# Gate and value products of layer 1 as a 2x2 block product with seven products, in the list scheduler's order

## The chip, the cores and the metric

One core of one Trainium2 chip runs the whole program. The metric is the time of one execution in device microseconds; three runs of a kernel give its median. Engine names: PE (TensorE, matrix products), DVE (VectorE), ACT (ScalarE), POOL (GpSimd), SP (SyncE, which here only issues DMAs). SBUF is the on-chip memory, PSUM the eight banks into which PE writes.

## What is computed

Attention with a threshold, then two layers in sequence. Cut to what matters here:

```
x = attention(q, k, v, tau)                  # 2304 tokens x 512
rms = sqrt(mean(x * x, axis=-1) + 1e-6)
xn = x / rms * rms_g
g = xn @ w_gate                              # 512 -> 1536
val = xn @ w_val                             # 512 -> 1536
x = (silu(g) * val) @ w_out                  # layer 1: 1536 -> 512
h = x @ w_in                                 # layer 2: 512 -> 2048
out = (h * cos(h)) @ w_out2                  # 2048 -> 512
```

Every factor is held as a high part (fp32r) and a low part (what is left), and a product is three matmuls: high by high, high by low, low by high.

## The kernel before

Tokens stand in six chunks of 384 (`TC`, `NCH`), with the model dimension on the partitions in four k-tiles of 128 (`KD`). Layer 1 has twelve column tiles of 128 for gate and value (`F1`), in six groups of two (`G1`). The loop goes over groups, in a group over chunks, in a chunk over the two tiles; one such step is a *unit* (72 in all, `seq`). A unit runs `gv_mm` twice, once for gate and once for value: four k-tiles by three matmuls each, 24 matmuls of 128x128 by 128x384 into tile `pgv` (two banks). Then ACT takes the silu (`h_silu`), DVE multiplies by value (`h_mul`), ACT makes the high part of h (`h_hi`) and DVE the low part (`h_lo`). `px_mm` multiplies h by the output weights: 12 matmuls into four banks `px`; after the second tile of a group `px_out` adds them to `acc`, in SBUF (four DVE adds of 128x384; in the first group four ACT copies).

Weights come as 64-bit floats. `weight_job` loads 512 KB (`raw`), turns it into 32 bit (two DVE steps, one ACT step and one POOL step on `wtmp`) and splits it (`whi` by ACT, `wlo` by DVE). Each weight tile is loaded and split once.

Two things set the order of the instructions. The attention, the first four units' gate and value products, the first two units' output products and the x of chunks 0 to 3 are steps of a `Plan`: a list scheduler with a cost in ns for each kind of step (`STEPS`), counted buffers (`take`, `free`), and a third number per kind that says which of the steps that could start goes first. It also keeps the steps in `LOCK` (DVE and POOL steps that use a common path to SBUF) from overlapping, by its own costs, and makes the POOL steps in `BEHIND` wait for the DVE step ahead. The rest of layer 1 and all of layer 2 are written out by hand: `pump` advances up to three weight jobs between units, and layer 1 sends unit n's output products behind unit n+1's gate and value products. Each engine works its own list in order; SP's DMAs are one queue.

Of the kernel before, what the change touches and what calls it, by code (L numbers as in the profile page):

```python
# [9 lines left out]
F32 = mybir.dt.float32  # L10
# [8 lines left out]
P = 128  # L19
# [57 lines left out]
    "j_a": ("ACT", 540, -8083508),
    "gv": ("PE", 2090, -3245104),
    "silu": ("ACT", 420, -5068320),
    "px": ("PE", 2090, 3553935),  # L80
    "pxc": ("ACT", 400, 54632),
    "hmul": ("DVE", 480, -8051011),
    "hhi": ("ACT", 420, -838003),
    "hlo": ("DVE", 480, 3843445),
# [5 lines left out]
    "mask", "j1", "j2", "x_d", "hlo", "th", "div", "sq", "x_add", "rms", "radd", "x_p", "j_p",  # L90
}
BEHIND = {"div", "sq", "x_add", "x_p", "j_p"}
# [9 lines left out]
N_EARLY = 4  # L102
N_PX = 2
# [111 lines left out]
def attention_moe_cos_kernel(  # L215
# [36 lines left out]
    w_a = ctx.enter_context(tc.tile_pool(name="w_a", bufs=6))  # L252
    x0_p = ctx.enter_context(tc.tile_pool(name="x0", bufs=1))
    xs = {}
# [41 lines left out]

    def weight_job(n, key, pool, stage, src, idle):
# [29 lines left out]
        hi = pool.tile([P, 4, P], F32R, tag="whi", name="whi")  # L327
        lo = pool.tile([P, 4, P], F32R, tag="wlo", name="wlo")
# [396 lines left out]
    def x_halves(c):  # L725
        if c not in xs:
            hi, lo = (late[c].tile([P, KD, TC], F32R, tag=t, name=t) for t in ("xh", "xl"))
            xs[c] = [(hi[:, kk], lo[:, kk]) for kk in range(KD)]
        return xs[c]
# [9 lines left out]
    def x_scale(c, kk):  # L739
        nc.gpsimd.tensor_tensor(acc[c, kk], acc[c, kk], xrs[c], op=ALU.mult)  # L740
# [87 lines left out]

    def px_out(g, c, d):
        dst = acc[c][:, d]  # L830
        if g == 0:
# [13 lines left out]

    def attention():
# [4 lines left out]
            "x0": 2, "jraw": 1, "jtmp": 1, "hh": 2, "one": 1,  # L851
        })
# [136 lines left out]
        def chunk(c, at, tiles, rs_tile, after, free):  # L989
# [6 lines left out]
            for kk in range(KD):  # L996
# [3 lines left out]
                x = add("x_p", at, x_scale, c, kk, after=[x, r])  # L1000
# [37 lines left out]
        def grow_2():  # L1038
            att_s.close()
            late[2] = ctx.enter_context(tc.tile_pool(name="xhl2", bufs=1, side="right"))  # L1040
            late["acc", 3] = late["acc", 0] = ctx.enter_context(
                tc.tile_pool(name="acc3", bufs=2, side="right")
            )
            late["rs", 3] = ss_p
# [10 lines left out]
        e2 = {}  # L1055

        def e_tile(i):
            if i not in e2:
                e2[i] = e_p.tile([P, 2, S], F32, tag="e", name="xe")
            return e2[i]  # L1060

        x2 = chunk(
            2, NU + 5, lambda kk: e_tile(kk // 2)[:, kk % 2, 0:TC], lambda: e_tile(2)[:, 0, 0:TC],
            [g2], [[("e", ("e2", 2))], [("e", ("e2", 0))], [], [("e", ("e2", 1))], [], [[]] * KD],
        )
        x = add("x_load", NU + 6, load_x, 3, after=[g2, done["rs", 2]] + x0 + [done[x] for x in range(8, 12)])
        add("x_p", NU + 6, scale_x, 3, after=[x])
        hs = []
        for n in range(N_EARLY):
            c = seq[n][1]  # L1070
            x = add("gv", NU + n, gv_mm, n, 0, after=(x0, x1)[c] + jops + [smm[NU - 1], g1],
                take=[(f"s{1 - n % 2}", ("gv", n))],
            )
            y = add("gv", NU + n, gv_mm, n, 1, after=[x])
            x = add("silu", NU + n, h_silu, n, after=[x, y], take=[("hh", ("hh", n))])
            x = add("hmul", NU + n, h_mul, n, after=[x, y], free=[("gv", n)])
            x = add("hhi", NU + n, h_hi, n, after=[x])
            hs.append(add("hlo", NU + n, h_lo, n, after=[x], free=[("hh", n)]))

        y = add("none", 999, lambda: acc.__setitem__(0, acc_tile(0, [P, KD, TC])), after=[g2])  # L1080
        z = None
        for n in range(N_PX):
            z = add("px", NU + n + 3, px_mm, n, after=[hs[n], z],
                take=[] if n else [("v", ("px", 0))] + [("t", ("px", d)) for d in range(1, KD)],
            )
# [5 lines left out]
    with tc.manual_schedule():  # L1091
# [49 lines left out]
        for _ in range(3):  # L1141
            pump(3)
# [166 lines left out]
```

## Time and profile before

| | us |
|---|---|
| three runs | 1165.12 median (1164.11 to 1166.32) |
| the profiled execution | 1162.08 |
| its span, first to last instruction | 1160.0 |
| PE busy in the span | 1140.5 |
| DVE busy | 819.6 |
| ACT busy | 653.6 |
| POOL busy | 320.7 |

The span lies 2.1 us under the time of its own execution. Busy times of engines overlap. Busy time of PE in a stretch equal to the stretch's length means that PE never waited there; a matmul's own duration overlaps the next one's, so its price is the distance between starts.

### The profile page before, as it was taken

To read this page: it belongs to the slowest core of one execution; us is meant where nothing else is said; L and a number is where in the kernel's file an instruction comes from. 1 tells how busy PE (TensorE), PEld (TensorE's weight loads), DVE (VectorE), ACT (ScalarE), POOL (GpSimd) and SP (SyncE) were. 2 spreads that over 40 slices of the span, in tenths; PEclk is the share of its full clock that TensorE was granted. 3 is DMA by queue.
4 is the path that set the end of the run, shared out by engine and by line. 5 is a ranking of instruction groups with operands and counts; after the bars stand their busy time and mean duration, and the time that the engine had idled before them with its cause. 6 is when DMAs were issued, how large, how long until landed. Compare 5 with 4: busy or idle time off the path is not lost.

```text
span 1160.0 us, 18700 instructions
## 1 busy us (share of the span) xinstructions
PE 1140.5 (98%) x7060; PEld 1033.4 (89%) x7060; DVE 819.6 (71%) x1595; ACT 653.6 (56%) x1234; POOL 320.7 (28%) x300
## 2 busy tenths in 40 slices
PE   8999999999899999999999999999999999999997
PEld 7777777777899999999999999989999999999995
DVE  7999999996484643725537347688697787867765
ACT  5888888887354312313213134487676676766663
POOL 1324255355542110201102002034233252332222
PEclk9999999999999999999999999999999999999999
DMA  5533453313533110301202103002012021100014
GB/s 125 127 94 94 112 121 93 87 53 101 169 99 109 55 55 1 109 1 37 73 1 70 40 1 110 1 17 90 4 39 70 1 73 37 37 1 1 1 55 109
DMA packets 99722, 71.69 MB, mean 62 GB/s; under 512 B 65296, under 2 KB 89648, under 8 KB 99632
## 3 DMA queue, kind: packets, MB, share of 16 engines
q1 hardware_dynamic: 98496, 70.20, 21.5%
q8 instruction: 56, 0.92, 0.3%
q10 hardware_dynamic: 1040, 0.26, 0.1%
q14 instruction: 34, 0.28, 0.1%
q0 software_dynamic: 96, 0.03, 0.0%
HBM read 60.95 MB, written 9.52 MB: 61 GB/s over the span
## 4 chain that ended last, share of the span: by engine, by line
PE 90%; DVE 4%; issue 3%; ACT 2%; POOL 0%; DMA 0%; SPq 0%; POOLq 0%
PE pgv L753 25%; PE ph L753 17%; PE po L753 16%; PE px L753 12%; PE po L647 7%; PE s L520 6%; PE pst L610 5%; ACT et L620 1%; DVE s L541 1%; PE psc L629 1%; DVE e L570 1%; PE psa L447 0%; DVE xl L747 0%; DVE wtmp L317 0%; DVE wtmp L312 0%
## 5 line engine op out<-in xcount | busy, mean ns | idle before, releaser
L753 PE MATMUL pgv<-xl,whi 128*128 128x384 f32 x576 | 194.5, 338 | 1.8 <-DVE xl L747 1.8
L753 PE MATMUL pgv<-xh,whi 128*128 128x384 f32 x576 | 194.4, 338 | 0.0
L753 PE MATMUL pgv<-xh,wlo 128*128 128x384 f32 x576 | 194.3, 337 | 0.0
L321 POOL TENSOR_TENSOR wtmp<-wtmp,raw 128x512 int32<-128x512 int32 x68 | 93.0, 1367 | 356.0 <-DVE wtmp L317 347.1
L1214 POOL TENSOR_TENSOR hlo<-r,hhi 128x384 fp32r<-128x384 f32 x96 | 98.1, 1021 | 304.0 <-ACT hhi L1213 248.0
L777 ACT ACTIVATE hh<-pgv 128x384 f32<-128x384 f32 x72 | 35.5, 493 | 249.9 <-PE pgv L753 249.9
L781 DVE TENSOR_TENSOR hh<-hh,pgv 128x384 f32<-128x384 f32 x72 | 39.7, 552 | 162.9 <-ACT hh L777 162.9
L753 PE MATMUL ph<-xh,whi 128*128 128x384 f32 x384 | 129.6, 338 | 0.0
L753 PE MATMUL ph<-xl,whi 128*128 128x384 f32 x384 | 129.5, 337 | 0.0
L753 PE MATMUL ph<-xh,wlo 128*128 128x384 f32 x384 | 129.2, 336 | 0.0
L1196 ACT ACTIVATE t<-ph,magic 128x384 f32<-128x384 f32 x96 | 55.8, 582 | 111.5 <-PE ph L753 111.5
L753 PE MATMUL po<-whi,hlo 128*128 128x512 f32 x288 | 114.6, 398 | 1.4 <-POOL hlo L1214 1.4
L753 PE MATMUL po<-whi,hhi 128*128 128x512 f32 x288 | 113.8, 395 | 0.2 <-ACT hhi L1213 0.2
L753 PE MATMUL po<-wlo,hhi 128*128 128x512 f32 x288 | 113.5, 394 | 0.0
L753 PEld LDWEIGHTS pgv<-xl,whi 128*128 128x128 f32 x576 | 108.6, 189 | 2.0 <-DVE xl L747 2.0
L753 PEld LDWEIGHTS pgv<-xh,whi 128*128 128x128 f32 x576 | 108.7, 189 | 0.6 <-issue 0.5
L753 PEld LDWEIGHTS pgv<-xh,wlo 128*128 128x128 f32 x576 | 108.7, 189 | 0.0
L560 ACT ACTIVATE e<-s,m 128x576 f32<-128x576 f32 x128 | 97.2, 795 | 15.6 <-DVE s L541 15.5
L570 DVE SCALAR_TENSOR_TENSOR e<-s,th,e 128x576 f32<-128x576 f32 x128 | 105.0, 849 | 0.9 <-POOL th L551 0.9
L1203 DVE SCALAR_TENSOR_TENSOR r<-t,r 128x384 f32<-128x384 f32 x96 | 99.1, 1032 | 3.3
L753 PE MATMUL px<-hlo,whi 128*128 128x384 f32 x288 | 97.9, 340 | 3.1 <-DVE hlo L789 3.1
L753 PE MATMUL px<-hhi,whi 128*128 128x384 f32 x288 | 97.9, 340 | 0.0
(129 smaller groups left out, 2585.4 us busy)
## 6 DMA issues: line engine op xcount, KB each, us to landing
raw<-in_moe_w_out_dram SPq DMA_DIRECT2D x28, 512.0 KB
raw<-in_moe_w_in_dram SPq DMA_DIRECT2D x16, 512.0 KB
raw<-in_moe_w_gate_dram SPq DMA_DIRECT2D x12, 512.0 KB
raw<-in_moe_w_val_dram SPq DMA_DIRECT2D x12, 512.0 KB
x<-xb SPq DMA_DIRECT2D x16, 288.0 KB
kn<-in_k_dram SPq DMA_DIRECT2D x16, 256.0 KB
vn<-in_v_dram SPq DMA_DIRECT2D x16, 256.0 KB
qn<-in_q_dram SPq DMA_DIRECT2D x15, 256.0 KB
```

The source lines that it names most:

```text
L321: nc.gpsimd.tensor_tensor(tmp, tmp, lw, op=ALU.add)
L520: nc.tensor.matmul(un[n]["ps", hd][:, c, 0:288], lhs, kh[bb][r, k0:k0 + 288], start=i == 0, stop=i == 2,)
L560: nc.scalar.activation(un[n]["e"][:, hd], un[n]["s", hd], AF.Exp, bias=grp[group_of(n)]["m"][:, c], scale=-1.0)
L570: nc.vector.scalar_tensor_tensor(e, un[n].pop(("s", hd)), grp[group_of(n)]["th"][:, ci:ci + 1], e, op0=ALU.is_le, op1=ALU.mult, accum_out= ...
L610: nc.tensor.transpose(ps[:, c], e[:, hd, k0:k0 + P], ident)
L647: nc.tensor.matmul(po[64 * hd:64 * hd + 64, :], vn[:, c, hd, :] if c < 4 else vl[:, hd, :], hf[j]["et"][:, hd, c, :] if c < 4 else hf[j][" ...
L753: nc.tensor.matmul(ps, w[a], x[bb], start=first and i == 0, stop=last and i == 2)
L777: nc.scalar.activation(hq[n], pgv[n][:, 0, 0:TC], AF.Silu)
L781: nc.vector.tensor_tensor(hq[n], hq[n], pgv.pop(n)[:, 1, 0:TC], op=ALU.mult)
L1196: nc.scalar.activation(t, ph, AF.Identity, bias=magic[:, 0:1], scale=INV2PI)
L1203: nc.vector.scalar_tensor_tensor(r, t, -C2, r, op0=ALU.mult, op1=ALU.add)
L1214: nc.gpsimd.tensor_tensor(lo, r, f(hi), op=ALU.subtract)
```

## The change

The gate weights (four k-tiles) and the value weights of a column tile are taken as a 2x2 block matrix: rows gate and value, columns k-tiles 0-1 and 2-3. Two chunks of x are the other 2x2 block matrix. The four results (gate and value of both chunks) then come from seven products in place of eight (Strassen's method in Winograd's form): `PROD` lists them. They need sums of weight quarters (`S24`, `S31` beside the plain `G` and `A22`) and differences of x quarters (`T1` to `T4`), which are split into high and low parts like the rest, and adds of the products afterwards, on DVE out of PSUM.

All of layer 1 is now in the `Plan`, with new kinds of steps and other numbers for the old ones. The first eight units (group 0, chunks 0 to 3) stay as they were. The remaining work goes in ten passes (`PASS`): groups 1 to 4 for the chunk pairs (0,1) and (2,3), group 5 for all three pairs, then groups 1, 0, 2, 3, 4 for the pair (4,5) alone. A block is one pass, one column tile and one pair: 32 blocks. Weights of groups 1 to 4 are stored to DRAM after the split and read again for the last passes; those of group 0 are converted a second time. The low half of h goes from DVE to POOL. Layer 2 takes the chunks in the order 2, 3, 0, 1, 4, 5. The core of the diff:

```diff
-    "pxc": ("ACT", 400, 54632),
+    "pr": ("PE", 990, 4800448),
+    "ra": ("DVE", 530, 79205),
...
-N_EARLY = 4
-N_PX = 2
+N_EARLY = 8
+LATER = 2800
...
-        nc.gpsimd.tensor_tensor(acc[c, kk], acc[c, kk], xrs[c], op=ALU.mult)
+        (nc.gpsimd if c < 2 else nc.vector).tensor_tensor(acc[c, kk], acc[c, kk], xrs[c], op=ALU.mult)
...
+    PAIRS = ((0, 1), (2, 3), (4, 5))
+    PASS = [(g, PAIRS[:2]) for g in range(1, len(G1) - 1)] + [(len(G1) - 1, PAIRS)] + [
+        (g, PAIRS[2:]) for g in (1, 0, 2, 3, 4)
+    ]
+    FIRST = len(G1) - 2
...
+        late["ps"] = late["m1s"].enter_context(tc.tile_pool(name="ps_c", bufs=4, space=PSUM, side="right"))
...
+        late["px"] = late["m1x"].enter_context(tc.tile_pool(name="ps_x", bufs=2, space=PSUM))
...
+                    G, sG = split("w", key("G"), part(gate, 0, 4), t + 4, [e0] + after["w"], [], save)
+                    A, sA = split("a22", key("A22"), part(val, 2, 4), t + 5, [e1] + after["a22"], [], save)
+                    ws = "ws" if m else "wt"
+                    s1 = add(ws, at(t + 6), op(part(val, 2, 4), part(val, 0, 2), part(val, 2, 4), ADD), after=[A])
+                    s3 = add(ws, at(t + 7), op(part(val, 0, 2), part(gate, 0, 2), part(val, 0, 2), SUB), after=[s1, e0])
+                    s2 = add(ws, at(t + 8), op(part(gate, 0, 2), part(val, 2, 4), part(gate, 0, 2), SUB), after=[s3, G])
+                    s4 = add(ws, at(t + 9), op(part(gate, 2, 4), part(gate, 2, 4), part(gate, 0, 2), SUB), after=[s2])
...
+                        x = again(tag, (m, j, u), (old, j, u), due(m, j) - 24 + d, [st[u]] + order[tag][-1:])
...
+            def y_add(cc):
+                y_tile(cc)
+                vec.tensor_tensor(y[cc], f(xt[cc][0]), f(xt[cc][1]), op=ADD)
...
+        PROD = (
+            ("p1", "G", 0, "B11"), ("p2", "G", 2, "B21"), ("p6", "S24", 0, "T2"), ("p5", "S31", 2, "T1"),
+            ("p7", "S31", 0, "T3"), ("p4", "A22", 0, "T4"), ("p3", "S24", 2, "B22"),
+        )
...
+                    for kk in range(2):
+                        mm3(ps[n], (w[0][:, a + kk], w[1][:, a + kk]), x[kk], kk == 0, kk == 1)
...
+            def lo(x, key):
+                return lambda: pool.tensor_tensor(H[key][1], tile_[x], f(H[key][0]), op=SUB)
...
+            r1 = add("rc", at(t0 - 60), lambda: act.copy(new("r1"), ps["p1"]), after=[steps["p1"]],
+                take=[("r", ("r", k, "r1"))], free=C("p1"))
+            a1 = plus("ra", "g1", "r1", "p2", 1, [r1], C("p2"), True)
+            s1 = add("rs", at(t0 - 58), lambda: act.activation(tile_["g1"], tile_["g1"], AF.Silu), after=[a1])
+            a2 = plus("ra", "r1", "r1", "p6", 2, [a1], C("p6"))
+            a3 = plus("ra", "vv", "r1", "p5", 3, [a2], C("p5"), True)
+            a4 = plus("ra", "r1", "r1", "p7", 4, [a3], C("p7"))
+            a5 = plus("ra", "v2", "vv", "p7", 5, [a3], C("p7"), True)
+            a6 = plus("ra", "r1", "r1", "p4", 6, [a4], C("p4"))
...
+            a7 = plus("ra", "vv", "vv", "p3", 8, [a5], C("p3"))
...
-            (g, c, i) for g in range(g1, g1 + len(G2)) for c in range(NCH) for i in groups[g][1]
+            (g, c, i) for g in range(g1, g1 + len(G2)) for c in (2, 3, 0, 1, 4, 5) for i in groups[g][1]
```

Where instructions stand, first on DVE in the middle of layer 1. Before, in a middle group (`hh`, `hlo`: multiply by value and low half of h; `acc<-acc,px`: output adds; `wtmp`: weight conversion):

```order
L317 SCALAR_TENSOR_TENSOR wtmp_6964<-raw_6907,wtmp_6964 128x512
L312 TENSOR_SCALAR wtmp_6969<-raw_6945 128x512
L781 TENSOR_TENSOR hh_6997<-hh_6997,pgv_6972 128x384
L789 TENSOR_TENSOR hlo_7001<-hh_6997,hhi_7000 128x384
L317 SCALAR_TENSOR_TENSOR wtmp_6969<-raw_6945,wtmp_6969 128x512
L834 TENSOR_TENSOR acc_5008<-acc_5008,px0_6947 128x384
L834 TENSOR_TENSOR acc_5008<-acc_5008,px1_6948 128x384
L834 TENSOR_TENSOR acc_5008<-acc_5008,px2_6949 128x384
L834 TENSOR_TENSOR acc_5008<-acc_5008,px3_6950 128x384
```

Of the change, in the passes of groups 1 to 4 (`r<-r,pc`, L1393: the adds of products; L1418 and L1424: the multiplies by silu; `acc<-acc,px`: output adds of 768 columns; `w`, `a`: low parts of weights):

```order
L1393 TENSOR_TENSOR r_5661<-r_5615,pc_5623 128x384
L1393 TENSOR_TENSOR r_5615<-r_5615,pc_5634 128x384
L1393 TENSOR_TENSOR r_5675<-r_5615,pc_5643 128x384
L1393 TENSOR_TENSOR r_5615<-r_5615,pc_5654 128x384
L1393 TENSOR_TENSOR r_5687<-r_5675,pc_5654 128x384
L1393 TENSOR_TENSOR r_5615<-r_5615,pc_5679 128x384
L1418 TENSOR_TENSOR r_5661<-r_5661,r_5615 128x384
L1083 TENSOR_TENSOR w_5670<-wtmp_5580,w_5670 128x512
L1083 TENSOR_TENSOR a_5697<-wtmp_5630,a_5697 128x256
L1324 TENSOR_TENSOR acc_5143<-acc_5143,px_5608 128x768
L1393 TENSOR_TENSOR r_5675<-r_5675,pc_5689 128x384
L1324 TENSOR_TENSOR acc_5143<-acc_5143,px_5702 128x768
```

The two steps per unit between weights and output adds have become chains of adds that read the product banks `pc`, one behind the other; the low half of h has left DVE.

Second, DVE at the start of layer 1, behind the attention's last mask. Before (`xl`: low half of x of chunks 1 and 2):

```order
L747 SCALAR_TENSOR_TENSOR xl_4564<-xe_4458,g_sb_85,xh_4563 128x384
L781 TENSOR_TENSOR hh_4597<-hh_4597,pgv_4548 128x384
L747 SCALAR_TENSOR_TENSOR xl_4564<-xe_4467,g_sb_85,xh_4563 128x384
L789 TENSOR_TENSOR hlo_4605<-hh_4597,hhi_4604 128x384
L781 TENSOR_TENSOR hh_4650<-hh_4650,pgv_4584 128x384
L789 TENSOR_TENSOR hlo_4658<-hh_4650,hhi_4657 128x384
L781 TENSOR_TENSOR hh_4692<-hh_4692,pgv_4637 128x384
L747 SCALAR_TENSOR_TENSOR xl_4717<-xe_4634,g_sb_85,xh_4716 128x384
L692 TENSOR_SCALAR r325_149<-pss_4719 128x5
L781 TENSOR_TENSOR hh_4725<-hh_4725,pgv_4679 128x384
```

Of the change (L1189: the sum of both halves of a whole chunk; L792 and L927: the scaling of chunks 2 and 3):

```order
L1189 TENSOR_TENSOR acc_4674<-xh_4534,xl_4535 128x1536
L833 TENSOR_TENSOR hh_4694<-hh_4694,pgv_4627 128x384
L792 TENSOR_TENSOR xe_4625<-xe_4625,xe_4621 128x384
L792 TENSOR_TENSOR xe_4642<-xe_4642,xe_4621 128x384
L792 TENSOR_TENSOR xe_4644<-xe_4644,xe_4621 128x384
L792 TENSOR_TENSOR xe_4649<-xe_4649,xe_4621 128x384
L799 SCALAR_TENSOR_TENSOR xl_4720<-xe_4625,g_sb_88,xh_4719 128x384
L927 TENSOR_TENSOR acc_4656<-acc_4656,rs_4654 128x384
L799 SCALAR_TENSOR_TENSOR xl_4720<-xe_4642,g_sb_88,xh_4719 128x384
L927 TENSOR_TENSOR acc_4656<-acc_4656,rs_4654 128x384 x2
```

The scaling of chunks 2 and 3, POOL's before, stands on DVE, and the whole-chunk sums stand between the first units' multiplies.

Third, POOL in the middle of layer 1. Before, only weight conversions:

```order
L321 TENSOR_TENSOR wtmp_5096<-wtmp_5096,raw_5071 128x512
L321 TENSOR_TENSOR wtmp_5224<-wtmp_5224,raw_5167 128x512
L321 TENSOR_TENSOR wtmp_5230<-wtmp_5230,raw_5205 128x512
L321 TENSOR_TENSOR wtmp_5267<-wtmp_5267,raw_5227 128x512
L321 TENSOR_TENSOR wtmp_5497<-wtmp_5497,raw_5472 128x512
L321 TENSOR_TENSOR wtmp_5535<-wtmp_5535,raw_5494 128x512
```

Of the change, about where the second excerpt of DVE stands (L1406: low half of h; L1124: the sums of weight quarters):

```order
L1054 TENSOR_TENSOR wtmp_5630<-wtmp_5630,raw_5505 128x512
L1406 TENSOR_TENSOR hlo_5711<-r_5661,hhi_5710 128x384
L1124 TENSOR_TENSOR wtmp_5630<-wtmp_5630 128x256
L1124 TENSOR_TENSOR wtmp_5630<-wtmp_5580,wtmp_5630 128x256
L1124 TENSOR_TENSOR wtmp_5580<-wtmp_5630,wtmp_5580 128x256
L1124 TENSOR_TENSOR wtmp_5580<-wtmp_5580 128x256
L1406 TENSOR_TENSOR h_5759<-r_5675,h_5759 128x384
L1054 TENSOR_TENSOR wtmp_5800<-wtmp_5800,raw_5672 128x512
L1054 TENSOR_TENSOR wtmp_5804<-wtmp_5804,raw_5699 128x512
L1406 TENSOR_TENSOR h_5862<-r_5757,h_5862 128x384
L1406 TENSOR_TENSOR hlo_5910<-r_5831,hhi_5909 128x384
```

The conversions now share POOL with the low halves of h and with four sums per column tile.

## Rows read from the trace of the kernel before

**Rows 1.** The page: busy us, share of the span, instructions.

```profile
span 1160.0 us, 18700 instructions
...
PE 1140.5 (98%) x7060; PEld 1033.4 (89%) x7060; DVE 819.6 (71%) x1595; ACT 653.6 (56%) x1234; POOL 320.7 (28%) x300
```

**Rows 2.** Windows: stretch, length, busy us (instructions) by engine, clock, DMA.

```profile
100.00:260.00 160.00, 159.36 (x1432) 123.01 (x1432) 154.10 (x409) 134.68 (x248) 70.36 (x73) 1.00 0.36 92
285.00:350.00 65.00, 60.17 (x338) 59.37 (x337) 41.85 (x51) 30.14 (x61) 34.70 (x23) 0.97 0.40 127
340.00:350.00 10.00, 10.00 (x49) 10.00 (x50) 8.69 (x15) 4.54 (x10) 2.63 (x2) 0.83 0.17 53
350.00:733.00 383.00, 383.00 (x2187) 383.00 (x2186) 199.78 (x353) 110.05 (x217) 44.53 (x34) 1.00 0.16 49
733.00:760.00 27.00, 26.58 (x149) 25.59 (x148) 16.04 (x30) 15.00 (x29) 1.00 (x1) 1.00 0.00 1
```

**Rows 3.** The chain that ended last, in layer 1: start, us, what.

```profile
347.80 4.16 PE pgv L753 x24
351.96 2.12 PE px L753 x12
```

**Rows 4.** Timeline of PE, 300 to 352: waits in brackets.

```profile
310.62 0.44 PE L753 MATMUL px<-hlo,whi 128*128 128x384 f32 x1 [3.06 <-DVE hlo L789]
...
339.85 0.60 PE L753 MATMUL pgv<-xl,whi 128*128 128x384 f32 x1 [1.77 <-DVE xl L747]
```

**Rows 5.** Timeline of DVE: start, us, line, operation, tile, shape, count.

```profile
276.29 0.81 DVE L570 SCALAR_TENSOR_TENSOR el<-s,th,el 128x576 f32<-128x576 f32 x1
...
310.02 1.01 DVE L789 TENSOR_TENSOR hlo<-hh,hhi 128x384 fp32r<-128x384 f32 x2
...
462.04 1.94 DVE L834 TENSOR_TENSOR acc<-acc,px 128x384 f32<-128x384 f32 x4
463.89 1.28 DVE L331 TENSOR_TENSOR wlo<-wtmp,whi 128x512 fp32r<-128x512 f32 x2
465.10 0.42 DVE L312 TENSOR_SCALAR wtmp<-raw 128x512 int32<-128x512 int32 x1
...
467.79 0.69 DVE L317 SCALAR_TENSOR_TENSOR wtmp<-raw,wtmp 128x512 int32<-128x512 int32 x1
```

**Rows 6.** Timeline of all engines, cut to DVE and POOL.

```profile
306.23 3.45 POOL L806 TENSOR_TENSOR acc<-acc,rs 128x1536 f32<-128x1536 f32 x1 [0.49 <-DVE xl L747]
...
306.42 3.67 DVE L747 SCALAR_TENSOR_TENSOR xl<-xe,g_sb,xh 128x384 fp32r<-128x384 f32 x1 [0.27 <-ACT xh L743]
...
468.71 1.30 POOL L321 TENSOR_TENSOR wtmp<-wtmp,raw 128x512 int32<-128x512 int32 x1 [55.42 <-DVE wtmp L317]
...
468.85 1.72 DVE L317 SCALAR_TENSOR_TENSOR wtmp<-raw,wtmp 128x512 int32<-128x512 int32 x1
...
472.59 0.54 DVE L781 TENSOR_TENSOR hh<-hh,pgv 128x384 f32<-128x384 f32 x1
...
472.90 1.31 POOL L321 TENSOR_TENSOR wtmp<-wtmp,raw 128x512 int32<-128x512 int32 x1 [0.78 <-DVE wtmp L317]
```

**Rows 7.** Groups by line and shape: busy us, mean ns, idle before.

```profile
L1203 DVE SCALAR_TENSOR_TENSOR r<-t,r 128x384 f32<-128x384 f32 x96 | 99.1, 1032 | 3.3
L1214 POOL TENSOR_TENSOR hlo<-r,hhi 128x384 fp32r<-128x384 f32 x96 | 98.1, 1021 | 304.0 <-ACT hhi L1213 248.0 <-issue 50.7 <-DVE acc L1254 3.2
...
L1207 DVE TENSOR_TENSOR r<-r,ph 128x384 f32<-128x384 f32 x96 | 52.0, 542 | 0.0
```

**Rows 8.** SP's timeline, one load; windows as in group 2.

```profile
470.04 0.37 SPq L307 DMA_DIRECT2D raw<-in_moe_w_gate_dram  x1
...
472.00:472.50 0.50, 0.50 (x5) 0.50 (x4) 0.50 (x1) 0.48 (x1) 0.12 (x1) 1.00 1.08 373
474.00:475.00 1.00, 1.00 (x8) 1.00 (x7) 1.00 (x2) 1.00 (x3) 0.21 (x1) 1.00 0.92 324
```

More of the change, by code (lines that the diff above doesn't have):

```diff
@@ new lines @@
+    "s": ("PE", 885, -6930363),
+    "s4": ("PE", 790, 1242378),
+    "warm": ("PE", 640, -112935),
+    "max": ("DVE", 680, -10255673),
+    "exp": ("ACT", 675, -1037703),
+    "th": ("POOL", 300, -1060633),
+    "mask": ("DVE", 742, -4138242),
+    "t": ("PE", 445, 57622),
+    "raw": ("ACT", 477, -6096088),
+    "c0": ("PE", 245, -608604),
+    "c1": ("PE", 465, -1489386),
+    "c_raw": ("ACT", 295, -1524940),
+    "radd": ("POOL", 250, -893656),
+    "rinv": ("DVE", 375, 3655923),
+    "r_out": ("SP", 2100, 2019715, 2500),
@@ new lines @@
+    "r_in": ("SP", 1700, -919170, 11000),
+    "av0": ("PE", 2212, -4109991),
+    "av1": ("PE", 2745, -1514959),
+    "avo": ("ACT", 300, -7631444),
+    "div": ("POOL", 1385, -204485),
+    "xout": ("SP", 500, 2015089, 2500),
+    "sq": ("POOL", 1122, 3600693),
+    "x_add": ("POOL", 1385, 166922),
+    "xsum": ("PE", 1085, 3874082),
+    "mean": ("DVE", 140, -6653549),
+    "rms": ("POOL", 1520, 56341),
+    "rs_out": ("SP", 2500, -3692696, 2500),
+    "x_load": ("SP", 500, 2189338, 6000),
+    "x_p": ("POOL", 1010, 5504962),
@@ L85 @@
+    "p1": ("PE", 990, 104910),
+    "rc": ("ACT", 470, 5448315),
+    "ra": ("DVE", 530, 79205),
+    "rs": ("ACT", 470, 111302),
+    "rm": ("DVE", 500, -7880511),
+    "rh": ("ACT", 480, -602101),
+    "rl": ("POOL", 1010, -3453313),
+    "po": ("DVE", 900, 47405),
+    "pq": ("ACT", 800, -3964306),
+    "wt": ("DVE", 350, -8454035),
+    "xhi": ("ACT", 830, -1549231),
+    "xlo": ("DVE", 880, 4230783),
 }
@@ L1054, in attention, with r_tile @@
         g2 = add("none", 999, grow_2, after=ends + x1)
[L1055 to L1060, printed above, removed]
+        gm = add("none", 999, grow_m, after=[g2] + [
+            s for s in plan.steps if s["kind"] in ("load_v", "exp", "mask", "t", "raw", "c0", "c1", "c_raw", "av0", "av1")
+        ])
+        def r_tile():
+            return late["r"].tile([P, TC], F32, tag="r", name="xe")
@@ L1081, in attention @@
[L1081 to L1085, printed above, removed]
-        for d in range(KD):
-            add("pxc", NU + 5, px_out, 0, 0, d, after=[z, y], free=[("v" if not d else "t", ("px", d))] if 0 else [("px", d)])
+            y = add("gv" + _, t + n, gv_mm, n, 1, after=[x], free=[("plw", n % 2)] * 2)
+            gvs.append(y)
@@ L1160, in attention_moe_cos_kernel @@
-        while done < len(seq):
-            next_o1()
-        xs.update(x2)
-        m1.close()
-        m2.close()
+        group[0] = len(G1)
+        finish_w2()
+        for c in (4, 5):
+            job = split_job(c)
+            flying.append([job, next(job)])
+        for n, (lay, fs, pool) in list(enumerate(groups))[len(G1) + 1:]:
+            for i in fs:
+                for kd in range(2):
+                    jobs.append((n, (str(lay), kd, i), late["odd" if n % 2 else "ring"], late["stage"], w2_src(kd, i), 4))
```

718 lines of the change are left out of this document (576 added, 142 removed).

## Prediction

> **What bounds the kernel now.** I read the busy table first: PE is busy 1140.5 of 1160.0 us, DVE 819.6 [rows 1]. So the question in every stage is whether PE can be kept supplied; an instruction taken from PE is worth its full length, one added to DVE, ACT or POOL is worth nothing until PE waits for it. Then I split the span. Layer 1 runs from 285 us (the last attention product) to about 748. Its dense part, 350 to 733, shows PE 383.00 us of 383.00 with 2187 matmuls [rows 2], one per 0.175 us; the chain gives the same per form, 4.16 us for 24 gate and value products (0.173) and 2.12 us for 12 output products (0.177) [rows 3]. DVE is busy 200 us there, ACT 110, POOL 45 [rows 2]. There is idle time only at the edges: 285 to 350 has 60.17 us of PE in 65 (4.8 us lost), in two waits for late DVE work of 3.06 and 1.77 us [rows 4], and from 340 to 350 the granted clock is 0.83, part of the time on the lower of its two levels, behind the second wait: another 10 x 0.17 = 1.7 us. The hand-over to layer 2 loses 0.4 us [rows 2].
>
> **PE: what goes.** The first eight of the 72 units (group 0, chunks 0 to 3) stay as they are. The other 64 become 32 blocks: one column tile of gate and value against two chunks. Eight quarter products become seven, each two k-tiles by three matmuls, so 42 instead of 48. The order lists agree: 6693 matmuls before, 6501 after. 192 x 0.175 = **33.6 us less** on the engine that sets the end. Shapes are unchanged (128x128 by 128x384), so I use the same pitch. A block then takes PE 42 x 0.173 + 24 x 0.177 = 11.5 us.
>
> **DVE: what comes, per block.** Starts of back-to-back instructions give the price: 1.94/4 = 0.485 us for 128x384 with a PSUM operand, 1.01/2 = 0.505 with both operands in SBUF, 1.28/2 = 0.64 for 128x512 [rows 5]; by that slope of 1.05 ns an element I estimate 0.91 for 768 columns, 0.37 for 256 and 1.7 for 1536. Each block has seven adds of a product (3.40), two multiplies (1.01) and two output adds of 768 columns (1.82). In the first 16 blocks (groups 1 to 4, pairs (0,1) and (2,3)) it also carries 1.5 weight conversions (0.42 + 0.69 each [rows 5], 1.67), two wide low parts (1.28) and half a narrow one (0.19). Sum 9.4 us of 11.5. Before, the two units that a block replaces cost DVE 4 x about 0.5 for the halves and 4 x 0.485 for the output adds, about 4 us without the weights. So DVE goes from half to four fifths full, and its cover is 2.1 us a block. ACT had 110 us in 383 and gets 78 instructions more in the whole program; even at 1 us each it stays at half.
>
> **The shared port.** DVE's two-input steps and POOL's do not run together. The L317 of 0.69 us took 1.72 when a POOL conversion started 0.14 us ahead of it, and an L747 took 3.67 under a POOL step of 3.45; but L781, which reads PSUM, and the POOL step that began inside it took their normal 0.54 and 1.31 [rows 6]. Layer 2 says the same on average: L1203 (two SBUF inputs) 1032 ns, L1207 (one in PSUM) 542 [rows 7]. The change gives POOL the low halves of h (2 x 1.02), 1.5 conversions (1.5 x 1.30) and two sums of weight quarters, between nothing and the 1.02 of 384 columns and by width about 0.7 each: 5.4 us a block. Port users are then POOL's 5.4 and DVE's 4.2 (multiplies 1.01, conversions 1.67, low parts 1.47), 9.6 of 11.5; DVE's other 5.2 us reads PSUM and can lie under POOL. It fits, if the order puts POOL's steps beside the PSUM adds. The order of the attention, made by the same scheduler, packs DVE 154 of 160 us with POOL at 70 and PE at 159.4 [rows 2], so I expect that it mostly does: **2 us** lost over these 16 blocks, bounds 0 and 16 (1 us each). The Trainium skill (SBUF — State Buffer, "Who interferes with whom") states an exclusive lock: a DVE instruction with two SBUF inputs and a GpSimd instruction that reads SBUF block each other fully, and whichever issues first holds. By that rule the delay falls on either engine, and a whole conversion can land on a DVE step that PE waits for; the 1.72 agrees, and the first rival prices it.
>
> **The start of layer 1.** Here most is added ahead of the first block: whole-chunk sums (1536 columns, three), the scaling of chunks 2 and 3 moved from POOL to DVE, the differences of x, the first weights. From the order, DVE has 42.9 us between the last softmax mask (which ended at 277.1 us [rows 5]) and the first add of a product; POOL has 4 x 1.02 (scaling), 6 x about 1.5 for 576 columns (by width from 1.02 for 384 [rows 7]) and 6 x 1.30: 21 us, and 38 us of DVE's also use the port. All in series: 277 + 38 + 5 + 21 = 341. PE comes to the first product after 192 + 48 matmuls, 285 + 41.8 = 327, and to the first one with a difference of x after 36 more, at 333. So between nothing lost (overlap as planned; DVE alone would be done at 320) and 8 us; behind the x loads it may be 14. I take 3.5 plus 1 for the clock, since part of POOL's work can lie where DVE waits for data, against 4.8 + 1.7 = 6.5 now: **2 us less**. Queued behind a late DVE step are the adds that free the four product banks; PE can go at most three products (3.1 us) beyond one that is not read, plus any output products that the order put between.
>
> **Transfers.** 40 stores and 40 loads of split weights (512 KB, a fifth of them 256) are new on SP's queue, with 6 more conversions. In a late pass, eight loads of 512 KB and two of 256 go within 23 us: 4.7 MB. The queue moved 324 GB/s over 1 us and 373 over half a us [rows 8], so 15 us of 23. One load: issued at 470.04, its last bytes move before about 473.3: 3.3 us. The output weights have two buffers only, and between the last output product of one pass and the first of the next PE has 18 to 24 products in the order, 3.1 to 4.2 us, plus one of 1.05. That is tight three times: **2 us**, bounds 0 and 9 (a whole load late each). Nothing of before shows the price of a store to DRAM beside loads; the nearest is the load's.
>
> **Hand-over, attention, layer 2.** Layer 2 starts with chunks 2 and 3, whose split is done some blocks earlier, but in banks of the last output products: 1.4 us in place of 0.4, bounds 0 and 4: **1 us more**. The attention has the same instructions in another order: 0, within 2. Layer 2's work is as before.
>
> **Sum.** 1160.0 - 33.6 - 2.0 + 2.0 + 2.0 + 1.0 = 1129.4 us of span. The profiled execution took 1162.1 for 1160.0; the median of the three runs is 3.0 above that. So 1131.5 as profiled, and I forecast **1135 us** beside the 1165.1.
>
> **Rivals.** (1) *The port decides, slower.* If every POOL step of the 16 blocks keeps DVE out, DVE needs 9.4 + 5.4 = 14.8 us a block, 3.3 more than PE: 53 us, and some 7 more at the start. 1129.4 - 2 + 53 + 7 = 1187 span, 1192 as a median. For it: the 1.72 and 3.67 rows, and POOL's steps wait for DVE's, so they fall where DVE is busy. Against it: the attention's packing. It decides when more than 2.1 + 33/16 = 4.2 of POOL's 5.4 us a block keep DVE out. (2) *DVE too tight in places.* The start loses 12 instead of 4.5, each of the 16 blocks 0.5, the reloads 6: 17.5 us more, 1147 span, 1152 median. For it: 1.0 us mean for the contended L1203 step [rows 7] where 0.5 is clean. (3) *Nothing lost.* Start 1, blocks 0, reloads 0, hand-over 0.4: 1160 - 33.6 - 6.5 + 1 = 1121 span, 1126 median. For it: a product on PE is 1.05 us, an add 0.49, and output products lie between. (4) *Reloads late.* If each of the ten late blocks waits 2.5 us for its weights, 25 - 2 more: 1152 span, 1157. Against it: 15 of 23 us.
>
> **Chances.** Forecast (1130 to 1143) 0.55; rivals 2 and 4 0.22; nothing lost 0.14; the port decides 0.07; no change within 0.2% 0.02 (gain just given back). The range 1126 to 1153 takes the forecast, half of rival 3 and most of rivals 2 and 4. A measurement of this kernel tells about 0.2% from no change: faster 0.91, same 0.02, slower 0.07.
>
> **What would show it.** Right: 1344 product matmuls and 1536 fewer gate/value ones; PE's wait for DVE's product adds under 0.3 us a block; DVE about 80 to 85% in the first 16 blocks; the conversion step of DVE near 0.7 us; layer 1 some 33 us shorter and the two other stages within 2 us. Wrong: PE waiting behind adds that stand in the queue behind a DVE step of 1.5 us or more (rival 1 or 2); PE waiting for a DMA at the first output product of a pass (rival 4); a granted clock under 1 in the middle of the layer; or a longer attention.

## The result, and the profile after

The changed kernel takes **1126.6 us** (median of four runs, 1124.69 to 1128.79), the kernel before, run beside it, 1164.6: a ratio of 0.968, 95% interval 0.965 to 0.970. It is 38.0 us faster; the forecast was 1135, some 30 faster, and 1126.6 is the time of rival 3, in which nothing is lost. The four runs spread over 4 us, so differences of a microsecond or two are not resolved.

The busy table of the changed kernel, to be laid beside [rows 1]:

```profile
span 1122.7 us, 19127 instructions
...
PE 1104.6 (98%) x6868; PEld 998.8 (89%) x6868; DVE 927.3 (83%) x1773; ACT 698.6 (62%) x1312; POOL 412.7 (37%) x411
```

PE lost 192 instructions and 35.9 us of busy time, DVE gained 107.7 and POOL 92.0, and PE still fills the span to 98%. The windows show where (columns as in [rows 2]: stretch, length, busy us and instructions of PE, PEld, DVE, ACT, POOL; clock; DMA share; GB/s):

```profile
285.00:350.00 65.00, 64.83 (x374) 64.21 (x371) 58.10 (x94) 38.01 (x77) 19.57 (x15) 1.00 0.50 167
345.00:531.00 186.00, 186.00 (x1061) 185.69 (x1060) 158.83 (x275) 83.48 (x163) 95.46 (x97) 1.00 0.47 164
600.00:709.20 109.20, 108.89 (x621) 108.33 (x620) 79.49 (x127) 35.25 (x65) 32.27 (x30) 1.00 0.54 179
709.20:736.00 26.80, 24.96 (x130) 22.84 (x130) 23.86 (x39) 22.23 (x44) 5.34 (x5) 1.00 0.02 3
```

The start of the layer has 374 matmuls in the 65 us that held 338 before, at full clock in place of 0.97. The second line has 16.1 blocks' worth of matmuls and holds most of the first 16 blocks: PE never waits, and DVE is busy 158.83 of 186, or 85%. The stretch of the reloads loses 0.31 us, the hand-over to layer 2 1.84. The first matmuls of a group on PE mark the ends of the layer, here of the changed kernel and then of the kernel before (columns: count, shortest, median and longest ns, first and last start):

```profile
L805 PE MATMUL pgv<-xh,w x128: 334/336/445, 285.3 to 326.4; 128*128 128x384 f32 x128
L805 PE MATMUL ph<-xh,w x768: 332/337/346, 709.0 to 1103.7; 128*128 128x384 f32 x192
```

```profile
L753 PE MATMUL pgv<-xh,whi x576: 334/334/525, 285.0 to 742.5; 128*128 128x384 f32 x192
L753 PE MATMUL ph<-xh,whi x384: 334/337/343, 747.6 to 1140.8; 128*128 128x384 f32 x192
```

Layer 1 lasts from 285.3 to 709.0, 423.7 us. Before, the same two groups began at 285.0 and 747.6: 462.6. So the layer is 38.9 shorter, the attention 0.3 longer and layer 2 1.3 longer. The list of what PE waited for over the whole program (us in total, times, longest) holds two entries of layer 1's block part, of 0.3 and 0.2 us:

```profile
PE po L805 <- ACT hhi L1824: 1.6, 2, 1.4
...
PE px L805 <- DMA w<-wd: 0.3, 1, 0.3
...
PE pc L805 <- DVE hh L833: 0.2, 1, 0.2
```

On DVE, the groups of the first 16 blocks (line, tile, count; busy us, mean ns; idle before):

```profile
L1393 DVE TENSOR_TENSOR r<-r,pc 128x384 f32<-128x384 f32 x115 | 61.6, 550 | 18.6 <-PE pc L805 12.6 <-ACT r L1409 2.8 <-ACT r L1423 0.7
L1324 DVE TENSOR_TENSOR acc<-acc,px 128x768 f32<-128x768 f32 x31 | 29.4, 949 | 4.1 <-PE px L805 3.9
L1083 DVE TENSOR_TENSOR w<-wtmp,w 128x512 fp32r<-128x512 f32 x32 | 22.4, 720 | 1.8 <-ACT w L1080 1.4 <-POOL acc L1198 0.3
L1049 DVE SCALAR_TENSOR_TENSOR wtmp<-raw,wtmp 128x512 int32<-128x512 int32 x23 | 15.0, 685 | 0.1
```

The conversion step (L1049, in the kernel before L317) runs at its clean 0.69 us of [rows 5], and DVE's idle time stands ahead of the product adds, waiting for PE: DVE waits for PE, not PE for DVE. The port that DVE and POOL share is not free of collisions: the first multiply of a block (L1418) takes 0.55 to 1.27 us in this stretch, 0.75 on average, where 0.55 is clean. But in this stretch none of them reaches PE.

### The profile page after: what moved, and what is told of

It is laid out like the page before. It is cut to its first block, busy times and chain, and to the rows that moved or that the text cites. A ratio compares the mean times of both kernels' runs of the same rounds, so it can differ in the third digit from the quotient of the medians.

```text
span 1122.7 us, 19127 instructions
## 1 busy us (share of the span) xinstructions
PE 1104.6 (98%) x6868; PEld 998.8 (89%) x6868; DVE 927.3 (83%) x1773; ACT 698.6 (62%) x1312; POOL 412.7 (37%) x411
## 4 chain that ended last, share of the span: by engine, by line
PE 89%; DVE 5%; ACT 2%; DMA 2%; issue 1%; POOL 0%; SPq 0%; POOLq 0%; DVEq 0%; ACTq 0%
PE pc L805 21%; PE ph L805 17%; PE po L805 17%; PE px L805 13%; PE po L698 7%; PE s L571 6%; PE pst L661 5%; DVE e L621 1%; DVE s L592 1%; DMA raw<-in_moe_w_gate_dram 1%; PE psc L680 1%; ACT et L671 1%; DMA w<-wd 0%; PE psa L498 0%; DMA k<-in_k_dram 0%
## 5 line engine op out<-in xcount | busy, mean ns | idle before, releaser
L805 PE MATMUL ph<-xh,w 128*128 128x384 f32 x768 | 212.0, 337 | 0.0
L805 PE MATMUL po<-w,hhi 128*128 128x512 f32 x576 | 180.4, 394 | 1.6 <-ACT hhi L1824 1.6
L1393 DVE TENSOR_TENSOR r<-r,pc 128x384 f32<-128x384 f32 x224 | 120.2, 551 | 45.6 <-PE pc L805 30.2
L805 PE MATMUL pc<-xh,w 128*128 128x384 f32 x512 | 146.2, 337 | 0.2 <-DVE hh L833 0.2
L805 PEld LDWEIGHTS ph<-xh,w 128*128 128x128 f32 x768 | 140.5, 188 | 3.9
L805 PE MATMUL ph<-xl,w 128*128 128x384 f32 x384 | 129.4, 337 | 0.0
L805 PEld LDWEIGHTS po<-w,hhi 128*128 128x128 f32 x576 | 107.0, 188 | 19.5 <-ACT hhi L1824 2.6
L805 PE MATMUL po<-w,hlo 128*128 128x512 f32 x288 | 114.2, 397 | 1.5 <-POOL hlo L1825 1.5
L805 PE MATMUL px<-h,w 128*128 128x384 f32 x516 | 102.4, 338 | 0.3 <-DMA w<-wd 0.3
L805 PEld LDWEIGHTS pc<-xh,w 128*128 128x128 f32 x512 | 94.1, 188 | 0.5 <-DVE hh L833 0.5
```

Of the source, the lines that this page charges most:

```text
L805: nc.tensor.matmul(ps, w[a], x[bb], start=first and i == 0, stop=last and i == 2)
L1393: vec.tensor_tensor(new(o) if fresh else tile_[o], src, ps[n], op=ADD)
```

## The experiments

One theory and its rivals at the outset. Theory A: PE sets layer 1, the gain is the matmuls that went plus the stall at the start of the layer that the new order removed, and DVE has room. The rivals: the order alone made the gain; DVE or the port is near its limit everywhere; the reloads are. Times are compared with the changed kernel's 1126.6; ratios are to the kernel before, whose median beside each set of runs was 1163.8 to 1164.9.

**The eighth product put back.**

```
-                    for kk in range(2):
+                    for kk in range(2) if n != "p1" else (0, 1, 0, 1):
                         mm3(ps[n], ..., kk == 0, kk == 1)
```

> The changed kernel with the first product of each of the 32 blocks computed twice into the same bank (the second time from a fresh start, so the output is the same): 48 product matmuls a block as before the change, everything else and the order as changed. Theory A (PE sets the layer, the gain is the matmuls that went): 192 x 0.175 = 33.6 us more than the changed kernel's 1126.6, so 1160, and the 4.5 us that still lack to the 1164.6 of before are the order at the start of the layer. Rival B (the order of the scheduler made the gain, the matmuls lay in PE's slack): under 1145. Rival C (PE waits for DVE in the blocks, so more time on PE gives DVE room): +20 to +28.

Measured: 1159.2 us, ratio 0.9957 (0.9939 to 0.9975): 32.6 us above the changed kernel, 0.170 us for each of the 192 matmuls. Its blocks:

```profile
345.00:531.00 186.00, 186.00 (x1063) 186.00 (x1062) 146.88 (x254) 77.00 (x152) 85.80 (x87) 1.00 0.45 160
```

PE is as full as with seven products. Within the noise every matmul that goes is gained at its full length, so in the changed kernel as it stands PE is the bound; rivals B and C fall out. It is still 4 to 5 us faster than the kernel before, and that rest belongs to the order: in the changed kernel's trace 36 more matmuls in the first 65 us of the layer are 6.3 us, less 1.4 at the hand-over and 0.3 in the attention.

**The kernel before, with three scalings moved to DVE.**

```
 def scale_x(c):
-    nc.gpsimd.tensor_tensor(
+    nc.vector.tensor_tensor(
```

> The kernel before, with one line changed: the three scalings of a whole chunk of x (1536 columns) run on DVE in place of POOL. Theory A (the changed kernel's gain beyond 33.6 us is the start of layer 1, where a POOL step of 3.45 us kept DVE out): 3 to 6.5 us faster than before, about 1160. Rival (DVE's whole load made the stall, not where the scaling ran): DVE gets 3 x 1.7 us more and the time stays within 1 us or rises by up to 3.

Measured: 1157.1 us, ratio 0.9945 (0.9929 to 0.996), 6.7 us faster than before. In its trace the start of the layer:

```profile
285.00:340.00 55.00, 53.54 (x311) 53.13 (x310) 31.07 (x47) 27.86 (x55) 20.95 (x18) 1.00 0.46 142
340.00:350.00 10.00, 10.00 (x58) 9.76 (x57) 8.04 (x12) 5.41 (x12) 5.55 (x3) 1.00 0.44 113
```

369 matmuls in the 65 us in place of 338 [rows 2], 5.4 us of PE, and the clock does not fall, since the wait ahead of it is gone; one wait of 1.5 us is left. The stall was POOL's long step: under the first scaling an L747 took 3.67 us [rows 6], and under the other two, in the kernel before, an L312 took 3.72 and an L331 3.98 (the first two lines are POOL's):

```profile
327.57 3.94 POOL L806 TENSOR_TENSOR acc<-acc,rs 128x1536 f32<-128x1536 f32 x1
334.90 3.81 POOL L806 TENSOR_TENSOR acc<-acc,rs 128x1536 f32<-128x1536 f32 x1
328.07 3.72 DVE L312 TENSOR_SCALAR wtmp<-raw 128x512 int32<-128x512 int32 x1
335.28 3.98 DVE L331 TENSOR_TENSOR wlo<-wtmp,whi 128x512 fp32r<-128x512 f32 x1
```

So 5 to 7 of the 38 us had nothing to do with the products: one line in the old kernel gives them.

**More work on DVE, five runs.** A block has three adds that write a fresh tile. They were issued again into the same tile, with the PSUM operand, or with the tile's SBUF operand twice:

```
     dst = new(o) if fresh else tile_[o]
+    for _ in range(r if fresh else 0):
+        vec.tensor_tensor(dst, src, ps[n], op=ADD)    # or (dst, src, src)
     vec.tensor_tensor(dst, src, ps[n], op=ADD)
```

Once more each, PSUM:

> The changed kernel with the three adds of a block that write a fresh tile issued twice (same inputs, a PSUM operand, same result): 3 x 0.485 = 1.46 us more of DVE in each of the 32 blocks, nothing else. Theory A (DVE has about 2 us a block free and its steps are not in PE's way): at most 4 us slower, DVE near 98% in the first 16 blocks. Rival 2 of the prediction (DVE is tight in places): 0.5 to 1 us a block in the first 16, 8 to 16 us slower. If DVE's steps were PE's bound throughout: 32 x 1.46 = 47 us slower.

Twice more each, PSUM:

> As the run with three repeated adds a block (14 us slower than the changed kernel), but each of the three issued three times: 2.9 us more of DVE a block. Theory A (a queue bound: the first 16 blocks become DVE's, 10.0 + 2.9 = 12.9 us in place of 11.7, the later ones have 11.4 and lose little): about 20 to 30 us slower than the changed kernel. Rival 2 (each step added ahead of an add that PE waits for is a wait of PE's): twice 14 or more, 28 to 45. If each added step lengthened PE's wait: 93.

Once more each, SBUF:

> As the run with three added DVE steps a block, but each added step has both operands in SBUF (the tile plus itself, overwritten at once by the true add): the same 1.5 us of DVE a block, now on the port that POOL's steps use. Theory A (the port has room, since POOL's and DVE's port steps come to 9.6 of 11.5 us and DVE's PSUM adds lie under POOL): no more than 5 us slower than the run with PSUM operands. Rival 1 of the prediction (the port decides): 11.1 of 11.5 us would be on the port, and the delays reach PE: 15 to 40 us slower than with PSUM operands.

The first of the three alone, PSUM and SBUF:

> The changed kernel with only the first of the fresh adds of a block issued twice: 0.49 us more of DVE a block, PSUM operand. With three such steps (1.46 us) the time rose by 14 us, with six (2.9) by 62. Theory D (there is a true margin of some 1 us a block, beyond which each 1 us costs 1 us): within 2 us of the changed kernel. Theory E (no margin: each step ahead of an add is a wait of PE's, in proportion): 14/3, about 5 us slower.

> As the run with one added step a block, with both operands in SBUF. Three such steps cost 35 us where three PSUM ones cost 14. Theory D (margin): the first step a block costs 2 to 6 us, since it also pushes POOL's steps on. In proportion: 35/3, about 12 us slower.

| added per block | us | over the changed kernel | ratio |
|---|---|---|---|
| one step, PSUM | 1128.2 | 1.6 | 0.9686 (0.9665 to 0.9707) |
| one step, SBUF | 1128.4 | 1.7 | 0.9689 (0.9668 to 0.9711) |
| three, PSUM | 1140.6 | 14.0 | 0.9803 (0.9784 to 0.9822) |
| three, SBUF | 1161.6 | 35.0 | 0.9975 (0.9963 to 0.9987) |
| six, PSUM | 1188.6 | 61.9 | 1.0209 (1.0189 to 1.0229) |

The first step costs next to nothing (its two intervals reach the changed kernel's 0.9676), so there is a margin; three are well beyond it. Theory A's "at most 4 us" for three was wrong; 14.0 is what rival 2 gave. Six cost more than either theory had for them (20 to 30, or 28 to 45) and less than if each were a wait of PE's (93). Windows of the run with three PSUM steps and of the run with six (for six also a later stretch):

```profile
345.00:531.00 186.00, 179.90 (x1008) 176.05 (x1007) 175.20 (x311) 80.55 (x157) 88.66 (x90) 1.00 0.46 160
```

```profile
345.00:531.00 186.00, 167.85 (x886) 159.64 (x885) 175.89 (x312) 71.88 (x141) 77.91 (x79) 0.96 0.44 154
550.00:650.00 100.00, 89.15 (x478) 82.43 (x478) 92.86 (x160) 37.24 (x70) 30.69 (x30) 1.00 0.24 79
```

DVE stops at 175 of 186 us, 94%, in both; most of the idle time that the trace puts down to an engine is short waits for ScalarE. A block has 66 matmuls, so the changed kernel's 1061 are 16.1 blocks of 11.57 us, with 158.83 / 16.1 = 9.9 us of DVE each. If 94% is the most that DVE reaches, the margin is not 11.57 - 9.9 = 1.7 us but 0.94 x 11.57 - 9.9 = 1.0 us. This is an estimate; the runs bracket it, between one step and three. Three steps of 0.55 pass it by about 0.6 us, 10 us over 16 blocks; the window has 53 matmuls fewer, 9.3 us. The other 4 to 5 us are lost behind 531 us, where PE waits in places although DVE is not full. With six a block takes 186 / (886 / 66) = 13.9 us, so the first 16 lose some 37 us, and DVE is full behind them too (92.86 of 100 us).

Three SBUF steps cost 21 us more than three PSUM ones, within rival 1's 15 to 40; theory A's "no more than 5" was wrong. The blocks' window of that run, and DVE's group of added steps from 330 to 620 us:

```profile
345.00:531.00 186.00, 170.41 (x923) 161.38 (x921) 174.44 (x285) 73.51 (x144) 87.34 (x81) 0.99 0.45 156
```

```profile
L1395 DVE TENSOR_TENSOR r<-r 128x384 f32<-128x384 f32 x66 | 53.7, 813 | 2.1 <-ACT r L1412 1.1
```

The added step takes 0.81 us on average in place of 0.55. POOL's conversion, 1.31 in the changed kernel, takes 1.43: the two meet on the port, and DVE needs 174.44 / (923 / 66) = 12.5 us a block. So rival 1's mechanism is there; with 1.5 us a block more on the port the gain is nearly gone.

**An order that is blind to POOL's hold of the port.** The scheduler's list LOCK names the kinds of step that it keeps apart; the layer's four POOL kinds were taken off it.

```
-    ... "wj1", "wj2", "wp", "ws", "wt", ... "tlo", "tr", "rm", "rl", "xlo",
+    ... "wj1", "wj2", "wt", ... "tlo", "rm", "xlo",
-BEHIND = {"div", "sq", "x_add", "x_p", "j_p", "wp", "ws", "tr", "rl"}
+BEHIND = {"div", "sq", "x_add", "x_p", "j_p"}
```

> The changed kernel with POOL's four kinds of step of this layer taken off the list of steps that the scheduler keeps apart from DVE's on the port, so the order is another one: same instructions, made blind to POOL's hold of the port. Theory A (PE sets the end; the order kept DVE's steps near their clean times, but there are 1.6 us a block to spare): DVE's low part of the weights goes from 0.71 toward 1.0 us, and the time rises by 2 to 8 us. Rival (the port-aware order is what makes the gain): 20 to 50 us slower. If the order doesn't matter: within 1 us.

Measured: 1146.0 us, ratio 0.9842 (0.9822 to 0.9861): 19.4 us given back, half of the change's gain. That is the edge of the rival's 20 to 50 and far above theory A's 2 to 8. DVE's groups from 330 to 620 us:

```profile
L1393 DVE TENSOR_TENSOR r<-r,pc 128x384 f32<-128x384 f32 x163 | 87.1, 547 | 9.2 <-ACT r L1409 2.8 <-PE pc L805 2.4
L1083 DVE TENSOR_TENSOR w<-wtmp,w 128x512 fp32r<-128x512 f32 x43 | 42.7, 1014 | 0.1
...
L1049 DVE SCALAR_TENSOR_TENSOR wtmp<-raw,wtmp 128x512 int32<-128x512 int32 x31 | 28.8, 931 | 0.2
L1424 DVE TENSOR_TENSOR r<-r 128x384 f32<-128x384 f32 x23 | 23.5, 1022 | 4.3 <-ACT r L1423 4.2
```

These three DVE steps with SBUF operands alone are longer (in the changed kernel, same stretch, 0.75, 0.71 and 0.61 us), the PSUM add is not (0.547). Not every step is: the first multiply, L1418, takes 0.67 in place of 0.70. The windows of the blind order:

```profile
330.00:345.00 15.00, 9.34 (x43) 8.54 (x42) 14.54 (x27) 7.59 (x15) 2.69 (x2) 0.77 0.74 255
345.00:531.00 186.00, 179.65 (x1016) 177.48 (x1015) 178.03 (x266) 80.38 (x157) 104.95 (x93) 1.00 0.47 160
```

In the blocks DVE is full (178.0 of 186), since the same steps take 178.03 / (1016 / 66) = 11.6 us a block in place of 9.9, and 45 matmuls fall out, 7.9 us. At the start of the layer 44 do (the changed kernel has 87 there), 7.7 us: one wait of 5.2 for a late low half of h, and the clock at 0.77 behind it. POOL's steps around that wait, and then the low half on DVE:

```profile
325.87 3.29 POOL L1054 TENSOR_TENSOR wtmp<-wtmp,raw 128x512 int32<-128x512 int32 x2 [7.91 <-ACT raw L1046]
338.23 1.39 POOL L1054 TENSOR_TENSOR wtmp<-wtmp,raw 128x512 int32<-128x512 int32 x1 [9.06 <-ACT w L1080]
337.91 0.56 DVE L841 TENSOR_TENSOR hlo<-hh,hhi 128x384 fp32r<-128x384 f32 x1
```

Most of the wait is the other order and not the port. POOL ran nothing between 329.2 and 338.2, and from 330.7 to 337.9 DVE worked 7.2 us of weight steps at their clean times ahead of that low half. Contention before that (the whole-chunk sum took 2.87 us in place of 1.75, a low part of differences 1.62 in place of 0.95) comes to 1.8 us at most.

**Twice the reload traffic.**

```
 def load():
+    spare = dram.tile(wd[old].shape, F32, ...)
+    dma(spare, wd[old])
     dma(f(tile_of(tag, key)), wd[old])
```

> The changed kernel with a copy of the same block in DRAM to a spare place in DRAM issued ahead of every load of split weights: the queue moves twice as much for them. Theory A (the loads are ahead of PE by about their own time; the output weights with two buffers by nothing: one of them came 0.3 us late with 5.4 us from issue to landing): the eight output loads of the late passes come 1 to 2 us late each, 8 to 16 us slower, and the product weights come in time. Rival 4 of the prediction (the loads are the near bound in the late passes): 30 us or more. If they have room: within 2 us.

Measured: 1139.9 us, ratio 0.9791 (0.9769 to 0.9813), 13.3 us slower. PE's waits from 345 us to the end of the layer:

```profile
PE px L805 <- DMA w<-wd: 7.9, 3, 4.8
PE pc L805 <- ACT r L1411: 1.8, 1, 1.8
```

The sum is as theory A gave it, the count is not: three output loads are late, not eight, by up to 4.8 us, and with ScalarE's 1.8 that is 9.7 us; the clock, 0.97 to 0.98 after 531 us, accounts for most of the rest. The product weights came in time. The output weights have no slack: in most of the runs here one output load was late, by 0.2 to 1.5 us, and in the blind order two were (2.6 together).

**Half of PE's products left out.**

```
-    for kk in range(2):
-        mm3(ps[n], (w[0][:, a + kk], w[1][:, a + kk]), x[kk], kk == 0, kk == 1)
+    mm3(ps[n], (w[0][:, a], w[1][:, a]), x[0], True, True)
```

> The changed kernel with each of the seven products over one k-tile in place of two (the second half of the inner dimension is left out): 21 matmuls a block fewer, 3.7 us of PE, so 8.0 us a block; DVE's work as it was. It asks what comes next behind PE. Queue theory: the first 16 blocks go down to DVE's 10.0 us, the later 16 to about 8.5: about 70 us faster than the changed kernel. After the runs with added DVE steps (a load of DVE that fitted cost 14 us already): the first 16 stay near 11, the later ones at 9 to 9.5: 40 to 50 us faster.

Measured in a single run: 1097.4 us, 29 faster, where PE has 32 x 3.68 = 118 us less to do. Even the later guess (40 to 50) was too high. In its trace PE waits for the product adds and for what ScalarE passes to them:

```profile
PE pc L805 <- DVE r L1392: 16.3, 23, 2.1
PE pc L805 <- ACT r L1408: 15.0, 10, 3.6
```

Its windows:

```profile
345.00:531.00 186.00, 153.37 (x771) 135.11 (x772) 170.00 (x295) 88.02 (x174) 100.96 (x101) 0.97 0.49 171
600.00:682.00 82.00, 72.00 (x359) 68.43 (x359) 64.73 (x105) 29.51 (x56) 23.94 (x22) 0.90 0.60 208
```

In the first 16 blocks DVE is busy 170.0 of 186 us and a block (45 matmuls now) takes 10.9 us in place of 11.57, about what the guess had. The late ones take 10.3, not 9 to 9.5: the clock is 0.90 there, and PE waits 5.6 us for reloads. So in the first 16 blocks of the changed kernel the next bound lies only some 0.7 us a block under the first.

**The hand-over to layer 2, twice.** First the splitting of the last two chunks was started four units later; then, on top of it, ScalarE's split of h was put ahead of the reduction of the newest unit for eight units:

```
+if n == 4:
+    for c in (4, 5): ...          # was ahead of the loop
+if n < 8 and 0 <= n - 3:          # second version only
+    split2(n - 3, r)
 pump(3, pool=0)
 if n < len(seq):
     in2(n)
     reduce2(n)
-if 0 <= n - 3 < len(seq):
+if 8 <= n and 0 <= n - 3 < len(seq):
     split2(n - 3, r)
```

> The changed kernel with the splitting of the last two chunks for layer 2 started four units later, so that ScalarE is not busy with it when the first h of layer 2 is due; same instructions. In the changed kernel PE waits 1.4 us for the first h and 0.4 for its low half. Theory A (ScalarE's queue makes this wait): 1.0 to 1.8 us faster, about 1125. Rival (the prediction's: the split waits for banks of the last output products, or the chain of the first h is that long by itself): within 0.4 us.

> The changed kernel with the splitting of the last two chunks four units later (as in the run before, where the first wait for h fell from 1.4 to 0.3 us but the second unit then waited 0.8) and, in the first eight units of layer 2, the halves of h ahead of the reduction of the newest unit on ScalarE, so that they do not wait for PE's newest product. If ScalarE's queue makes the waits: both go, 1.5 to 2 us faster than the changed kernel, PE busy over 26.3 of the 26.8 us behind the hand-over in place of 24.96. If not: within 0.4 us.

Measured: 1126.5 (ratio 0.9678) and 1125.0 us (0.9662, 0.9642 to 0.9681). PE's waits around the hand-over in the first version, 1.9 us in all, as much as in the changed kernel:

```profile
PE po L805 <- ACT hhi L1821: 1.1, 2, 0.8
PE po L805 <- POOL hlo L1822: 0.8, 2, 0.4
```

The first wait fell to 0.3 us and the second unit got one of 0.8: ScalarE used the room for weights, and the time stayed within the rival's 0.4 us. In the second version:

```profile
709.20:736.00 26.80, 26.27 (x138) 24.11 (x137) 20.80 (x36) 21.02 (x39) 8.71 (x7) 1.00 0.14 40
```

PE is busy 26.27 us in place of 24.96, so the order of ScalarE's queue was the cause of these waits. That the whole program gains by it is not shown: against the changed kernel the intervals overlap, and in its profiled run an output load that was 1.5 us late took the 1.3 back (span 1122.9).

## Why the prediction was right, point by point

The mechanism was right: PE sets the layer and what goes from it is gained. The size was not: 38.0 us came where 30 were forecast. The time lies outside the 1130 to 1143 that had 0.55 of the chances, in rival 3, which had 0.14, and 0.6 us above the lower end of the range; that it is inside at all is partly luck.

- **PE, 33.6 us less**: right. With the eighth product back, 32.6.
- **The start, 2.0 us less**: right in sign, mis-sized, and the term with most of the error. 36 more matmuls fit into its 65 us, 6.3 us; I had left 4.5 of the old 6.5 standing and 0.2 stands. The step that failed is "between nothing lost and 8 us, I take 3.5 plus 1 for the clock": the order keeps POOL's 21 us mostly apart from DVE's port steps, the collisions that are left cost PE no more than 0.2, and with no long wait the clock stays at 1.00. Another order can lose what I feared (the blind one loses 7.7 us in 15), but mostly by what it puts ahead in DVE's queue; two engines in series on the port, as I had reckoned the upper bound, is not what the runs show there.
- **The 16 blocks, 2.0 us**: mis-sized, 0. DVE at 85% (forecast 80 to 85), no wait for a product add, the conversion at 0.69. But "its cover is 2.1 us a block" was too wide: it is about 1.0 by the estimate above, since DVE has 9.9 us a block instead of 9.4 and stops at 94% under added steps.
- **The shared port**: the mechanism was right, and "if the order puts POOL's steps beside the PSUM adds" was the right condition. Made blind to it, the order gives 19.4 us back. The Trainium skill (SBUF — State Buffer, "Who interferes with whom") states that a DVE instruction with two SBUF inputs contends with a GpSimd instruction that reads SBUF. The trace of the blind order agrees for most: the weights' low parts and the second multiply grew to 1.01 and 1.02 us, PSUM adds, which have one SBUF input, stayed at 0.55; the first multiply did not grow. That rival 1 did not come is owed in part to the order. There was little room: 1.5 us a block more on the port cost 35 us. But even the blind order lost only a third of rival 1's 60: DVE's blocks grew by 1.7 us each, where the rival had all of POOL's 5.4.
- **Reloads, 2.0 us**: 0.3 in the profiled run. "Tight" was right: doubled traffic costs 13.
- **Hand-over, 1.0 us more**: 1.84 against 0.4, 1.4 more. The size was about right and the reason wrong: PE waited for ScalarE's half of h, and the order of ScalarE's queue made that wait, not the banks.
- **Attention and layer 2**: 0.3 and 1.3 us, within the 2 us given; the 1.3 is the hand-over.

The three loss terms that did not come are the start's 4.3, the blocks' 2.0 and the reloads' 1.7: 1129.4 - 8.0 + 0.4 for the hand-over + 0.3 for the attention is 1122.1, and the span is 1122.7. All three were guesses between a lower bound of nothing and a larger one, and all three came out at the lower bound. The evidence for the lower bound was there: the attention, ordered by the same scheduler, keeps PE at 159.4 of 160 with DVE at 154 [rows 2].

## What to carry to other kernels

Take the gain apart: put the removed work back under the new order (here 32.6 us), and mend the old order's worst stall in the old kernel (6.7 us, one line). Measure a helper engine's margin by adding steps to it instead of reading it off its idle share: 15% idle was about 9% usable by the estimate above (5% was added for some 2 us), and the same three steps cost 35 us in place of 14 where they share a port. When a cut on the bound engine is paid for by work on another, the next cut is worth little: here 118 us less on PE, with DVE's work as it was, gave 29.

## What I had not expected of the hardware

Over 160 or 186 us DVE never got beyond 94 to 96%: 94% with three or six added steps, 96% in the blind order and in the attention [rows 2]. And a DVE step with one SBUF input and a constant waits for POOL too. The prediction speaks of "two-input steps", but its sum of port users has this step in it, and so has `LOCK`. Timeline of the changed kernel, cut to three steps:

```profile
328.62 1.30 POOL L1054 TENSOR_TENSOR wtmp<-wtmp,raw 128x512 int32<-128x512 int32 x1 [4.15 <-DVE acc L1189]
328.87 1.34 DVE L1040 TENSOR_SCALAR wtmp<-raw 128x512 int32<-128x512 int32 x1
...
330.24 0.69 DVE L1049 SCALAR_TENSOR_TENSOR wtmp<-raw,wtmp 128x512 int32<-128x512 int32 x1
```

The L1040 takes 0.42 us alone [rows 5, as L312]; here it began 0.25 us after a POOL conversion and ended 0.29 us after it. In the blind order its mean rose to 0.63 (0.46 in the changed kernel). The L312 of 3.72 us under a POOL scaling of 3.94, above, is the same thing in the kernel before.
